# A sparse-attention and mixing kernel: the order of all five instruction streams written by a list scheduler of its own, and GpSimd's pieces halved

## The chip, the cores and the metric

One core of a Trainium2 chip runs the whole program. The metric is the device time of one execution in microseconds (us), the median of several runs. The engines have these names: PE (TensorE, matmuls and transposes), PEld (its weight loads, which overlap with matmuls), DVE (VectorE), ACT (ScalarE), POOL (GpSimd), and SP, whose queue issues DMAs.

## The reference, cut to what matters

```python
scores = q @ k.T / sqrt(64)                  # 8 batches, 8 heads, 576 x 576
thresh = max(scores, -1) - tau
attn = softmax(where(scores >= thresh, scores, -1e9))
x = concat_heads(attn @ v)                   # (8, 576, 512)
theta = x @ w_theta                          # 512 x 512
zr, zi = x * cos(theta), x * sin(theta)
u = x + w_tok_r @ zr + w_tok_i @ zi          # over the 576 tokens
out = u + relu(u @ w_ch)                     # 512 x 512
```

The four weight matrices arrive as eight-byte numbers, all else as float32.

## The kernel before, in words

**Attention.** Two heads of one batch form a pair; there are 32 pairs, four for each batch. A pair is worked in nine halves: four tiles of 128 query rows for either head, and a ninth that holds the last 64 rows of both. A half is a chain over three engines. PE makes the scores `s_ps` (L288: four matmuls of 288 columns, ten in the ninth half). `s_ps` has one buffer, so the next scores wait until DVE has copied these to `sc` (L292, which takes the row maximum on the way). A small addition makes the threshold (L306 on POOL for batches 0 and 1, L310 on DVE later), ACT takes the exponential (L314), and DVE masks and sums (L318). PE transposes the half (L344, four transposes, and L359, a fifth for the last 64 keys of every second half) into a PSUM bank of the pool `ps_t` with its six banks, ACT copies that to `a` (L349), and after four and after nine halves PE multiplies with `v` (L379, two groups of 20 instructions). `normalize` spreads the reciprocals of the row sums over partitions (L395) and multiplies them on (L401). The products want float32 accuracy, so `q`, `k`, `x`, `u` and `z` are split into a rounded high part and a low part, the difference. The low parts of `q` (L238) and `k` (L114, tile k) are made on POOL but for the first pair, those of `x` and `u` (L114, tiles xl and ul) on POOL for three chunks in four and on DVE for the fourth.

**Mixture.** For every batch, once its four pairs are there: `angle` (L423, tiles m_ps<-xh and xl; four chunks m of 24 matmuls), `sines` (L485 to L508: the absolute value on DVE, two sines on ACT between two table loads, the products with x on POOL as L507), `flip` (L519, transposes with a high and a low part, L521 and L522), `token` (L536, four chunks of 54 matmuls), `split_u`, and the last product (L423, tiles m_ps<-uh and ul) with its eviction L584 and the store L589. `ORDER` sets the steps.

**Weights.** `load_weight` turns the eight-byte numbers of 17 chunks (four of `w_theta`, nine of the two token matrices, four of `w_ch`) into high and low parts with five DVE instructions (L142 to L151), and three matmuls (L166 to L168) for 13 of the chunks. The pieces of `w_theta` and `w_ch` go to DRAM and come back through `get_wm` (L202), a DMA on POOL's queue.

**What sets the order.** PE's order is written out by hand: the main loop at the end starts the scores of a half three halves ahead (`AHEAD`), and `fill` puts in so much of the mixture of the batch before that it is spread evenly over the 36 halves of a batch (`share`). The other engines' orders come from the framework's scheduler by priorities (`ATTENTION`, `SINES`) and estimates of its own.

Of the kernel before, what the change touches and what calls it, by code (L numbers as in the profile page):

```python
# [39 lines left out]
def tile_attn_moe(  # L40
# [17 lines left out]
    SP = S + 64  # L58
    NK = 9

# [4 lines left out]
    ps_t = ctx.enter_context(tc.tile_pool(name="ps_t", bufs=6, space=PSUM))  # L65

    @contextmanager
    def at(offset, step=1):

        here = tc.cur_priority  # L70
        tc.cur_priority = max(0, here + offset)
        yield
        tc.cur_priority = here + step
# [3 lines left out]

# [11 lines left out]
    span = small[:, 2 : 3]  # L89
    nc.vector.tensor_scalar(out=gate, in0=tau_sb, scalar1=0.0, scalar2=1.0 / root, op0=ALU.is_ge, op1=ALU.mult)  # L90
    nc.vector.tensor_scalar(out=span, in0=tau_sb, scalar1=0.0, scalar2=BIG, op0=ALU.is_lt, op1=ALU.mult)
    nc.vector.tensor_tensor(out=span, in0=tau_sb, in1=span, op=ALU.add)
    half_pi = small[:, 3 : 4]
    nc.vector.memset(half_pi, 0.5 * math.pi)
# [5 lines left out]
    def pool_copy(out, in_):  # L100
        nc.gpsimd.tensor_scalar(out=out, in0=in_, scalar1=1.0, scalar2=0.0, op0=ALU.mult, op1=ALU.add)

    def copy(eng, out, in_):
        if eng is nc.scalar:
            nc.scalar.copy(out=out, in_=in_)  # L105
        elif eng is nc.gpsimd:
            pool_copy(out, in_)
        else:
            eng.tensor_copy(out=out, in_=in_)  # L109

    def split(eng_hi, eng_lo, hi, lo, src):

        copy(eng_hi, hi, src)
        eng_lo.tensor_tensor(out=lo, in0=src, in1=hi.bitcast(F32), op=ALU.subtract)  # L114

    def temp(name, dt=F32):
        return pool.tile([P, S], dt, tag="t576", name=name, bufs=4)

    def after(ins, other):

        info = mybir.DependencyInfo(mybir.DependencyClass.NoSync, mybir.DependencyReason.DATA)
        tc.add_manual_dep(ins.ins, other.ins.name, info, reason="order")
        return ins

    turn = [0, 0]
    table = SimpleNamespace(back=None, exps=[])

    def load_weight(src, n, places, on_pe):

        raw_tag = turn[0] % 2  # L130
        turn[0] += 1
        tag, bufs = ("z", 3) if raw_tag else ("wm", 3)
        raw = pool.tile([P, S, 2], U32, tag=tag, name="wraw", bufs=bufs)[:, :n]
        nc.sync.dma_start(raw, src.bitcast(U32).rearrange("p (n t) -> p n t", t=2))
        low, high = raw[:, :, 0], raw[:, :, 1]
        w = pool.tile([P, S], F32R if on_pe else F32, tag="xh", name="w", bufs=4)[:, :n]
        bits = pool.tile([P, S], U32, tag="xh", name="bits", bufs=4)[:, :n]
        mag = pool.tile([P, S], U32, tag="xl", name="mag", bufs=4)[:, :n]
        magf, bitsf = mag.bitcast(F32), bits.bitcast(F32)
        yield  # L140
        nc.scalar.activation(out=magf, in_=high.bitcast(F32), func=AF.Abs)
        nc.vector.tensor_scalar(out=magf, in0=magf, scalar1=W_LEAST, scalar2=W_MOST, op0=ALU.max, op1=ALU.min)  # L142
        yield
        nc.vector.tensor_scalar(
            out=bits, in0=mag, scalar1=3, scalar2=0x3FFFFFFF, op0=ALU.logical_shift_left, op1=ALU.bitwise_and
        )
        nc.vector.scalar_tensor_tensor(
            out=bits, in0=high, scalar=0xC0000000, in1=bits, op0=ALU.bitwise_and, op1=ALU.bitwise_or
        )
        nc.vector.tensor_scalar(out=mag, in0=bits, scalar1=0xFF800000, scalar2=None, op0=ALU.bitwise_and)  # L150
        nc.vector.scalar_tensor_tensor(out=w, in0=low, scalar=2.0**-52, in1=magf, op0=ALU.mult, op1=ALU.mult)  # L151
        if not on_pe:
            nc.vector.tensor_tensor(out=w, in0=w, in1=bitsf, op=ALU.add)
            yield
            hi, lo = places()
            split(nc.scalar, nc.vector, hi, lo, w)
            return
        yield

        hi, lo = places()  # L160
        nc.scalar.copy(out=hi, in_=bitsf)
        n2 = n if n <= 512 else n // 2
        for c in range(0, n, n2):
            r = slice(c, c + n2)
            ps = ps_t.tile([P, 512], F32, tag="t", name="w_ps")[:, :n2]
            nc.tensor.matmul(ps, ident, bitsf[:, r], start=True, stop=False)  # L166
            nc.tensor.matmul(ps, one, w[:, r], start=False, stop=False)
            nc.tensor.matmul(ps, minus, hi[:, r], start=False, stop=True)  # L168
            nc.scalar.copy(out=lo[:, r], in_=ps)

    def load_wtok(c):
        yield from load_weight(w_tok[c * P : (c + 1) * P, :], S, lambda: (wt_h[:, c], wt_l[:, c]), True)

    def load_wm(which, src, c):
        kept = []

        def places():
            kept.extend(
                pool.tile([P, DM], F32R, tag="zh4" if x == "whi" else "zl4", name=x, bufs=4) for x in ("whi", "wlo")
            )  # L180
            return kept

        yield from load_weight(src[c * P : (c + 1) * P, :], DM, places, which == 0)
        for i, t in enumerate(kept):
            nc.sync.dma_start(
                wm_dram[which, :, :, i, c, :].rearrange("m p e -> p m e"),
                t.bitcast(F32).rearrange("p (m e) -> p m e", e=P),
            )

    def all_loads(todo):  # L190
        for fn, a in todo:
            yield from fn(*a)

    loads = [(load_wm, (0, w_theta, c)) for c in range(NM)]
    loads += [(load_wtok, (c,)) for c in range(NK)]
    streams = [all_loads(loads[i::2]) for i in range(2)]

    late = all_loads([(load_wm, (1, w_ch, c)) for c in range(NM)])

    def get_wm(which, m):  # L200
        t = pool.tile([P, 2, NM, P], F32R, tag="wm", name=f"wm{which}", bufs=3)
        nc.gpsimd.dma_start(t, wm_dram[which, m].bitcast(F32R))  # L202
        return t

    qq_t = []
    for i in range(2):
        qq = const.tile([P, S + SP], F32R, name=f"qq{i}")
        nc.gpsimd.memset(qq[:, S:SP].bitcast(F32), 0.0)
        qq_t.append(qq)
# [6 lines left out]

    xT = {}
    pairs = {}

    def load_raw(n, src, name, j):  # L220
        raw = temp(name)
        for r in (slice(0, 64), slice(64, P)):
            nc.sync.dma_start(raw[r], src[n // NP, n % NP, :, j])
        return raw

    def prepare_q(n, heads=(0, 1)):

        if 0 in heads:
            pairs[n] = SimpleNamespace(n=n, b=n // NP, p=n % NP, keys=[], a={})
        pr = pairs[n]  # L230
        pr.qf = qq_t[n % 2]
        for j in heads:
            raw = load_raw(n, qT, f"qraw{n}", j)
            qq = pr.qf[:, SP * j : SP * j + S]
            nc.scalar.activation(out=raw, in_=raw, func=AF.Copy, scale=gate)  # L235
            nc.scalar.copy(out=qq, in_=raw)  # L236
            eng = nc.gpsimd if n else nc.vector
            eng.tensor_tensor(out=qq[64:128], in0=raw[64:128], in1=qq[64:128].bitcast(F32), op=ALU.subtract)  # L238

# [62 lines left out]
    def softmax(u, j):  # L302
# [12 lines left out]
        if table.back is not None:  # L315
            after(ins, table.back)
# [409 lines left out]
```

## Time and profile before

| what | value |
|---|---|
| median of 3 runs | 1108.44 us (1106.35 to 1109.0) |
| the profiled execution | 1106.87 us, its span from first to last instruction 1105.1 us |
| first scores copied, first matmul of a mixture | 9.1 us, 135.58 us |
| from one batch's first `sc` to the next, batches 2 to 6 | 128.3 to 129.2 us |
| after the last `sc` | 81.5 us |
| granted clock of TensorE, mean | 0.995 of full speed |

The profiled execution's own time is 1.8 us above its span. The stages below are bounded by the first `sc` of a batch: 9.1, 122.8, 255.1, 383.8, 512.1, 641.3, 769.8, 898.2 us, and the last one at 1023.6 us. From the second stage on each stage holds the attention of one batch and most of the mixture of the batch before; after 1023.6 us only mixtures are left.

### The profile page before, as it was taken

What the parts mean: (1) busy time and instruction counts of PE and PEld (TensorE: products, weight loads), DVE (VectorE), ACT (ScalarE), POOL (GpSimd) and SP (SyncE); (2) the same over time, 40 slices, a digit from 0 to 9 for tenths busy, and PEclk for the clock granted to TensorE, in tenths of its full rate; (3) what the DMA queues carried; (4) which work ended last, traced back from release to release, by engine and by line L of the source; (5) the groups of instructions that cost most, each with busy time, mean ns of one, the idle gap of its engine ahead of it and who ended that gap; (6) DMA issues with size and microseconds to landing.
All of it is one profiled execution on the core that took longest, in us unless ns stands there. A gap on an engine that the chain in (4) does not pass through costs nothing.

```text
span 1105.1 us, 21156 instructions
## 1 busy us (share of the span) xinstructions
PE 1030.0 (93%) x7736; PEld 913.7 (83%) x7736; DVE 844.8 (76%) x2070; ACT 740.4 (67%) x1402; POOL 426.8 (39%) x375
## 2 busy tenths in 40 slices
PE   4888899899999999999999999999999999899998
PEld 3666688698788888888878988898888888788898
DVE  6898787976886679767887778876797668877472
ACT  6788878566786568765686667964687656864350
POOL 3345645444352343532363243522435323630210
PEclk9999999999999999999999999999999999999999
DMA  8632222345221243314232152212432143300411
GB/s 267 198 109 87 76 79 84 98 131 169 84 85 55 67 147 101 87 34 125 90 100 66 33 173 80 85 54 70 145 106 82 33 134 98 90 28 1 138 58 62
DMA packets 55175, 105.25 MB, mean 95 GB/s; under 512 B 11936, under 2 KB 20128, under 8 KB 55072
## 3 DMA queue, kind: packets, MB, share of 16 engines
q1 hardware_dynamic: 45856, 70.35, 21.3%
q0 software_dynamic: 9216, 33.56, 10.3%
q8 instruction: 61, 1.00, 0.4%
q14 instruction: 42, 0.34, 0.1%
HBM read 90.24 MB, written 13.63 MB: 94 GB/s over the span
## 4 chain that ended last, share of the span: by engine, by line
PE 64%; DVE 14%; ACT 10%; issue 5%; POOL 3%; DMA 2%; SPq 0%; POOLq 0%; ACTq 0%; DVEq 0%
PE y_ps L536 16%; PE m_ps L423 14%; PE s_ps L288 12%; PE o_ps L379 10%; PE t_ps L344 7%; DVE sc L292 3%; DVE s_sb L318 3%; DVE th L474 2%; PE z_ps L519 2%; ACT s_sb L314 1%; ACT qraw L235 1%; POOL k L114 1%; POOL qq L238 1%; PE t_ps L359 1%; DMA qraw<-in_qT_dram 1%
## 5 line engine op out<-in xcount | busy, mean ns | idle before, releaser
L318 DVE SCALAR_TENSOR_TENSOR s_sb<-sc,nm,s_sb 128x576 f32<-128x576 f32 x288 | 265.2, 925 | 81.0 <-ACT s_sb L314 70.7
L314 ACT ACTIVATE s_sb<-sc,nm 128x576 f32<-128x576 f32 x288 | 223.8, 780 | 103.7 <-DVE sc L292 102.8
L288 PE MATMUL s_ps<-k,qq 128*128 128x288 f32 (+1 forms) x1344 | 240.0, 306 | 52.1 <-DVE sc L292 34.0
L292 DVE TENSOR_SCALAR_CACHE_REDUCE sc<-s_ps 128x576 f32<-128x576 f32 x288 | 216.9, 753 | 68.8 <-PE s_ps L288 64.6
L288 PEld LDWEIGHTS s_ps<-k,qq 128*128 128x128 f32 x1344 | 194.1, 192 | 79.5 <-DVE sc L292 43.6
L349 ACT COPY a<-t_ps 128x512 f32<-128x512 f32 x256 | 148.5, 580 | 61.0 <-PE t_ps L344 60.2
L344 PE MATMUL t_ps<-ident,s_sb 128*128 128x128 f32 x1152 | 175.3, 275 | 0.8 <-DVE zl L522 0.8
L379 PE MATMUL o_ps<-a,v 128*64 128x320 f32 (+1 forms) x1280 | 170.0, 411 | 1.0 <-ACT a L349 0.8
L536 PE MATMUL y_ps<-wt_h,zh 128*128 128x288 f32 x576 | 164.7, 304 | 1.2 <-ACT zh L521 1.2
L536 PE MATMUL y_ps<-wt_l,zh 128*128 128x288 f32 x576 | 163.3, 302 | 0.0
L114 POOL TENSOR_TENSOR k<-kraw,k 128x576 fp32r<-128x576 f32 x62 | 93.9, 1515 | 165.2 <-ACT k L105 163.6
L344 PEld LDWEIGHTS t_ps<-ident,s_sb 128*128 128x128 f32 x1152 | 142.6, 142 | 1.5 <-DVE zl L522 1.0
L379 PEld LDWEIGHTS o_ps<-a,v 128*64 128x64 f32 x1280 | 86.4, 136 | 62.7 <-issue 6.4
L238 POOL TENSOR_TENSOR qq<-qraw,qq 64x576 fp32r<-64x576 f32 x62 | 99.8, 1612 | 60.0 <-ACT qq L236 29.2
L536 PEld LDWEIGHTS y_ps<-wt_h,zh 128*128 128x128 f32 x576 | 108.7, 189 | 1.7 <-ACT zh L521 1.7
L536 PEld LDWEIGHTS y_ps<-wt_l,zh 128*128 128x128 f32 x576 | 108.9, 189 | 0.0
L202 POOL DMA_DIRECT2D wm<-wm_dram x64 | 36.3, 568 | 179.2 <-PE m_ps L423 144.5
L536 PE MATMUL y_ps<-wt_h,zl 128*128 128x288 f32 x576 | 103.2, 305 | 0.0
L507 POOL TENSOR_TENSOR z<-z,xT 128x576 f32<-128x576 f32 x56 | 84.3, 1536 | 20.3 <-ACT z L494 20.1
L423 PE MATMUL m_ps<-xh,wm 128*128 128x288 f32 x512 | 90.6, 303 | 0.3 <-ACT xh L105 0.3
L114 POOL TENSOR_TENSOR ul<-xT,uh 128x576 fp32r<-128x576 f32 x24 | 34.8, 1448 | 132.5 <-DVE uh L109 89.2
L423 PE MATMUL m_ps<-uh,wm 128*128 128x288 f32 x512 | 84.0, 299 | 0.0
(89 smaller groups left out, 1663.9 us busy)
## 6 DMA issues: line engine op xcount, KB each, us to landing
wm<-wm_dram POOLq DMA_DIRECT2D x64, 512.0 KB, 3.7
qraw<-in_qT_dram SPq DMA_DIRECT2D x128, 144.0 KB, 3.0
kraw<-in_kT_dram SPq DMA_DIRECT2D x128, 144.0 KB, 2.9
out_dram<-xT SPq DMA_DIRECT2D x32, 288.0 KB, 2.1
v<-in_vp_dram SPq DMA_DIRECT2D x32, 256.0 KB, 2.7
wraw<-in_w_tok_dram SPq DMA_DIRECT2D x9, 576.0 KB, 4.3
wraw<-in_w_theta_dram SPq DMA_DIRECT2D x4, 512.0 KB, 6.5
wm_dram<-whi SPq DMA_DIRECT2D x8, 256.0 KB, 2.4
```

The lines of the kernel that those rows point to most:

```text
L114: eng_lo.tensor_tensor(out=lo, in0=src, in1=hi.bitcast(F32), op=ALU.subtract)
L238: eng.tensor_tensor(out=qq[64:128], in0=raw[64:128], in1=qq[64:128].bitcast(F32), op=ALU.subtract)
L288: nc.tensor.matmul(ps[:, h, d0:d1], st, kk, start=(x == 0), stop=(x == len(todo) - 1))
L292: nc.vector.tensor_scalar(out=sc.rearrange("p (a b) -> p a b", a=2), in0=ps[:, :, :HS], scalar1=-1.0, scalar2=None, op0=ALU.mult, op1=ALU.min,
L314: ins = nc.scalar.activation(out=e, in_=u.ps[j], func=AF.Exp, bias=nm[:, j : j + 1], scale=-1.0)
L318: nc.vector.scalar_tensor_tensor(out=e, in0=u.ps[j], scalar=nm[:, 2 + j : 3 + j], in1=e, op0=ALU.is_le, op1=ALU.mult, accum_out=u.pr.rows[ ...
L344: nc.tensor.transpose(out=tp[:, c * P : (c + 1) * P], in_=u.sf[:, k0 + c * P : k0 + (c + 1) * P], identity=ident)
L349: nc.scalar.copy(out=t.a[:, :, j, q0 : q0 + P], in_=tp.rearrange("p (c q) -> p c q", c=4))
L379: nc.tensor.matmul(o[64 * j : 64 * j + 64, :w], st, mv, start=(c == 0), stop=(c == 4))
L423: nc.tensor.matmul(tiles[h][:, :HS], wm[:, a, c, :], parts[c][bb][:, hs], start=(count[h] == 0), stop=(count[h] == 11))
L507: lo_eng.tensor_tensor(out=zi, in0=zi, in1=x, op=ALU.mult)
L536: nc.tensor.matmul(ps[:, :HS], z, w, start=(n == 0), stop=(n == len(work) - 1))
```

## The change

Every piece of work becomes an `Op` with its engine, a duration, a key (when it is wanted, counted in halves) and the buffers that it reads and writes. `Plan.run` goes through time: of the operations that are ready on an engine within 0.04 us of the earliest it takes the one with the lowest key, and emits all five engines' instructions in that order. The table `AT` holds the keys' offsets. A rule `held_up` adds to the key of an operation of DVE or POOL (those marked `lock`) that would collide with one of the other. Buffers have explicit slots; `s_ps` still has one, `ps_t` still six banks, and raws, row reciprocals and the halves of the `w` chunks share three buffers.

What moves between engines: the low parts of `k` and `u`, two of four of `x`, and those of `q` for pairs 0 to 5 go to DVE, and so do the 72 small additions of POOL (L306). POOL keeps the low parts of `q` from pair 6 on, two of four of `x`, and the products with the sines of batches 0 to 6, each as two instructions of 288 columns. ACT takes all of the evictions to `th` (two chunks of four were DVE's, L465). The absolute value becomes a bit operation. The 64 loads of `get_wm` go from POOL's queue to SP's. The four chunks of `w_ch` are added up on PE as the others are.

```diff
-AHEAD = 3
-ATTENTION, SINES = 20, 10000
-LAG = 3
+SEM = 0.06
+TABLE = 1.29
+AT = {
+    "wait": 0.04, "margin": 0.0, "held": 2.51,
...
+    "pq": 26, "px": 2, "pu": 0, "pz": 7, "pk": 0, "ta": 4, "cut": 2,
+}
+def ON_POOL(what, n, j):
+    if what == "q":
+        return n >= 32 - AT["pq"]
+    if what == "k":
+        return j < AT["pk"]
+    if what == "x":
+        return j < AT["px"]
+    if what == "u":
+        return j < AT["pu"]
+    return n < AT["pz"]
...
+class Plan:
...
+    def run(self):
...
+        while todo:
+            best = None
+            for e in range(5):
+                got = [(t, o) for o in cand[e] if forced[e] in (None, o) and (t := begin(o)) is not None]
...
+                t0 = min(t for t, _ in got)
+                _, t, o = min(((o.key + AT["held"] * held_up(o, t, AT["margin"]), o.n), t, o) for t, o in got if t <= t0 + AT["wait"])
+                if best is None or t < best[0]:
+                    best = (t, o)
...
+        self.ops.sort(key=lambda o: (o.start, o.n))
+        for o in self.ops:
+            o.fn()
...
+    def low(on_pool, out, in0, in1, key, R, W, n=S):
...
+        (b, p), k = W, AT["cut"]
+        if on_pool:
+            for i in range(k):
+                gps(c_pool(n // k), lambda i=i: go(nc.gpsimd, S * i // k, S * (i + 1) // k), key, R, ((b, (p, i)),))
+        else:
+            dve(c_two(n), lambda: go(nc.vector), key, R, ((b, [(p, i) for i in range(k)]),), lock=True)
...
-        nc.gpsimd.dma_start(t, wm_dram[which, m].bitcast(F32R))
+        load(lambda: nc.sync.dma_start(t().bitcast(F32), wm_dram[which, m]), key, (wm_b[which],), (t,), 512)
...
-    with tc.manual_schedule(engines={nc.tensor.engine}):
...
+    with tc.manual_schedule(engines={e.engine for e in (nc.tensor, nc.vector, nc.scalar, nc.gpsimd, nc.sync)}):
+        plan.run()
```

**SP's queue at the start.** Before, the `k` of the second head of pair 0 is the fourth load:

```order
L223 DMA qraw_97<-in_qT_dram 64x576 x2
L223 DMA kraw_103<-in_kT_dram 64x576 x2
L223 DMA qraw_110<-in_qT_dram 64x576 x2
L223 DMA kraw_116<-in_kT_dram 64x576 x2
L134 DMA wraw<-in_w_theta_dram 128x1024
```

Now:

```order
L477 DMA raw<-in_qT_dram 64x576 x2
L477 DMA raw<-in_kT_dram 64x576 x2
L477 DMA raw<-in_qT_dram 64x576 x2
L510 DMA v<-in_vp_dram 128x512
L513 DMA v_91<-in_vp_dram 64x64 x2
L366 DMA wm<-in_w_theta_dram 128x1024
L510 DMA v<-in_vp_dram 128x512
L513 DMA v_93<-in_vp_dram 64x64 x2
L477 DMA raw<-in_kT_dram 64x576 x2
```

The second head's `k` has moved behind the `v` of two pairs and the first chunk of `w_theta`.

**DVE where the third mixture begins**, some 400 us into the program. Before, the low part of the fourth chunk of `x` (xl, L114) stands between two `sc`, and a mask (L318) follows ahead of the next `sc`:

```order
L292 TENSOR_SCALAR sc,nm<-s_ps 128x576
L114 TENSOR_TENSOR xl<-xT_4605,xh 128x576
L310 TENSOR_SCALAR nm<-nm,small 128x1
L318 SCALAR_TENSOR_TENSOR s_sb,rows_4670<-sc,nm,s_sb 128x576
L292 TENSOR_SCALAR sc,nm<-s_ps 128x576
L318 SCALAR_TENSOR_TENSOR s_sb,rows_4670<-sc,nm,s_sb 128x576
```

Now, at the same place, with the scores of the same pair:

```order
L578 SCALAR_TENSOR_TENSOR s_4936,rows<-sc,nm,s_4936 128x576
L347 TENSOR_TENSOR xl<-xT,xh 128x576
L558 TENSOR_SCALAR sc,nm<-s_ps 128x576
L347 TENSOR_TENSOR xl<-xT,xh 128x576
L566 TENSOR_SCALAR nm<-nm,small 128x1
L578 SCALAR_TENSOR_TENSOR s_5030,rows<-sc,nm,s_5030 128x576
L558 TENSOR_SCALAR sc,nm<-s_ps 128x576
L566 TENSOR_SCALAR nm<-nm,small 128x1
L578 SCALAR_TENSOR_TENSOR s_5030,rows<-sc,nm,s_5030 128x576
L558 TENSOR_SCALAR sc,nm<-s_ps 128x576
L347 TENSOR_TENSOR k<-raw,k 128x576
```

There are two low parts of `x` now, one ahead of and one behind the `sc`, and a low part of `k` follows.

**PE at that place.** Before, only three matmuls with xl stand between a transposed half and the next scores, and these three need a low part:

```order
L423 MATMUL m_ps<-xh,wm_4945 128x288 x12
L344 MATMUL t_ps<-ident,s_sb 128x128 x4
L359 MATMUL t_ps<-ident,s_sb 128x128
L423 MATMUL m_ps<-xl,wm_4945 128x288 x3
L288 MATMUL s_ps<-k_12_1_4528,qq_87 128x288
```

Now:

```order
L745 MATMUL m_ps<-xh,wm 128x288 x9
L550 MATMUL s_ps<-k,qq_87 128x288 x4
L745 MATMUL m_ps<-xh,wm 128x288 x3
L745 MATMUL m_ps<-xl,wm 128x288 x6
L597 MATMUL t_ps<-ident,s_5030 128x128 x4
L745 MATMUL m_ps<-xh,wm 128x288 x2
L745 MATMUL m_ps<-xl,wm 128x288
L550 MATMUL s_ps<-k,qq_87 128x288 x6
```

The scores have moved into the middle of the matmuls with xh, and the six with xl stand together behind them.

## Rows read from the trace of the kernel before

**Rows 1.** The page's first part: busy us of each engine, its share of the span, and instructions.

```profile
PE 1030.0 (93%) x7736; PEld 913.7 (83%) x7736; DVE 844.8 (76%) x2070; ACT 740.4 (67%) x1402; POOL 426.8 (39%) x375
```

**Rows 2.** Busy time by stretch. The columns: stretch in us, its length, busy us of PE, PEld, DVE, ACT and POOL with their instructions, granted clock, DMA share, GB/s.

```profile
9.00:122.80 113.80, 91.45 (x564) 70.92 (x564) 98.63 (x224) 92.52 (x180) 55.20 (x58) 0.99 0.52 158
122.80:135.58 12.78, 10.82 (x76) 8.00 (x75) 10.20 (x28) 12.16 (x26) 7.06 (x8) 1.00 0.25 71
135.58:255.10 119.52, 110.48 (x824) 98.30 (x823) 98.44 (x215) 79.17 (x148) 56.66 (x62) 0.97 0.32 93
...
255.10:1023.60 768.50, 740.15 (x5713) 663.52 (x5712) 594.11 (x1519) 526.13 (x999) 293.24 (x223) 1.00 0.29 87
...
383.80:512.10 128.30, 123.72 (x958) 111.06 (x957) 99.20 (x255) 88.61 (x168) 50.19 (x38) 1.00 0.30 89
...
1000.00:1020.00 20.00, 20.00 (x156) 18.18 (x156) 14.41 (x39) 8.76 (x19) 1.42 (x1) 1.00 0.00 1
...
1023.60:1105.10 81.50, 75.54 (x563) 71.98 (x562) 41.13 (x79) 25.33 (x45) 13.35 (x15) 0.99 0.28 88
```

**Rows 3.** Links of the chain that ended last, from 1000 us on, where PE is never idle: start in us, length in us, engine, tile, line, and how many instructions are merged.

```profile
1002.03 0.44 PE t_ps L344 x4
1002.58 0.79 PE y_ps L536 x6
...
1005.91 2.84 PE o_ps L379 x20
1008.76 0.59 PE rb_ps L395 x4
1009.45 0.53 PE s_ps L288 x4
...
1019.92 2.31 PE o_ps L379 x20
1022.23 1.35 PE s_ps L288 x10
...
1088.47 12.75 PE m_ps L423 x96
```

**Rows 4.** What PE waited for in the stage from 383.8 to 512.1 us: us in total, times, longest.

```profile
PE s_ps L288 <- DVE sc L292: 1.9, 3, 0.9
PE t_ps L359 <- DVE zl L522: 1.1, 1, 1.1
PE s_ps L288 <- POOL k L114: 1.0, 1, 1.0
PE rb_ps L395 <- DVE km L468: 0.6, 1, 0.6
```

**Rows 5.** The timeline where the third mixture begins, from three answers (PE, DVE, POOL): start in us, length, engine, line, and in brackets the idle time before with what ended it.

```profile
403.96 0.92 PE L423 MATMUL m_ps<-xl,wm 128*128 128x288 f32 x3
405.80 0.80 PE L288 MATMUL s_ps<-k,qq 128*128 128x288 f32 x4 [0.91 <-DVE sc L292]
...
401.14 1.95 DVE L114 TENSOR_TENSOR xl<-xT,xh 128x576 fp32r<-128x576 f32 x1
...
403.13 1.93 DVE L318 SCALAR_TENSOR_TENSOR s_sb<-sc,nm,s_sb 128x576 f32<-128x576 f32 x1
...
406.71 0.82 DVE L318 SCALAR_TENSOR_TENSOR s_sb<-sc,nm,s_sb 128x576 f32<-128x576 f32 x1
...
403.00 1.43 POOL L114 TENSOR_TENSOR xl<-xT,xh 128x576 fp32r<-128x576 f32 x1
```

**Rows 6.** Groups of DVE instructions over the whole run, shapes kept apart: busy us, mean ns of one, idle us before them.

```profile
L318 DVE SCALAR_TENSOR_TENSOR s_sb<-sc,nm,s_sb 128x576 f32<-128x576 f32 x288 | 265.2, 925 | 81.0 <-ACT s_sb L314 70.7 <-POOL nm L306 5.0 <-ACT qraw L235 0.5
...
L310 DVE TENSOR_SCALAR nm<-nm,small 128x1 f32<-128x1 f32 x216 | 44.8, 208 | 2.4
...
L114 DVE TENSOR_TENSOR xl<-xT,xh 128x576 fp32r<-128x576 f32 x8 | 17.0, 2129 | 1.2 <-ACT xh L105 1.2
...
L114 DVE TENSOR_TENSOR ul<-xT,uh 128x576 fp32r<-128x576 f32 x8 | 6.1, 759 | 0.3
...
L150 DVE TENSOR_SCALAR mag<-bits 128x512 uint32<-128x512 uint32 x8 | 3.4, 419 | 0.0
```

**Rows 7.** Groups of DVE instructions from 9 to 135.58 us: the three one-input steps of the weights' conversion, the same columns.

```profile
L144 DVE TENSOR_SCALAR bits<-mag 128x576 uint32<-128x576 uint32 (+1 forms) x13 | 7.7, 591 | 1.1 <-PE w_ps L166 1.1
L142 DVE TENSOR_SCALAR mag<-mag 128x576 f32<-128x576 f32 (+1 forms) x13 | 7.1, 544 | 2.4 <-ACT mag L141 2.4
L150 DVE TENSOR_SCALAR mag<-bits 128x576 uint32<-128x576 uint32 (+1 forms) x13 | 7.0, 537 | 0.1
```

**Rows 8.** The start: busy time from 10 to 15 us (columns as in rows 2), and the fourth load in SP's queue (start and length of its issue).

```profile
10.00:15.00 5.00, 2.54 (x7) 1.90 (x8) 4.29 (x9) 2.81 (x4) 1.01 (x2) 1.00 0.96 243
...
4.95 1.24 SPq L223 DMA_DIRECT2D kraw<-in_kT_dram  x2
```

**Rows 9.** The timeline of PE where a converted chunk of 512 columns is added up, with what follows it.

```profile
44.48 1.02 PE L166 MATMUL w_ps<-bits,ident 128*128 128x512 f32 x2
...
45.80 0.60 PE L344 MATMUL t_ps<-ident,s_sb 128*128 128x128 f32 x4
```

**Rows 10.** The timeline where the last mixture begins: DVE's low part of `x`, and PE behind POOL's.

```profile
1040.86 3.67 DVE L114 TENSOR_TENSOR xl<-xT,xh 128x576 fp32r<-128x576 f32 x1 [1.03 <-ACT xh L105]
...
1043.96 0.80 PE L423 MATMUL m_ps<-xl,wm 128*128 128x288 f32 x4 [0.95 <-POOL xl L114]
```

More of the change, by code (lines that the diff above doesn't have):

```diff
@@ L27 @@
 W_MOST = 122880.0 - 2.0**-7
-AHEAD = 3
-ATTENTION, SINES = 20, 10000
-LAG = 3
-ORDER = "a0 a1 s01 a2 a3f0 s23 t0f1 t1f2 t2f3 t3"
+PE, DVE, ACT, POOL, SP = range(5)
+SEM = 0.06
+TABLE = 1.29
+AT = {
+    "wait": 0.04, "margin": 0.0, "held": 2.51,
+    "theta": 4.0, "theta_by": 4.33, "tok": 24.0, "tok_by": 1.7, "ch": 52.0, "ch_by": 3.89,
+    "q": -7.95, "k": -7.06, "raw": -2.0, "v": -4.0, "m0": 5.11, "m1": 4,
+    "score": -1.5, "nm": -1.4, "add": -1.39, "exp": -2.3, "mask": -1.0, "wrap": -1.58, "turn": -0.16, "copy": 0.05, "last": 0.06,
+    "v0": 4.5, "v1": 9.2, "vcopy": 1.1, "div": 9.4, "rows": -2.22, "rb": -1.5, "dmul": 0.16,
[3 rows of a table added]
+}
@@ new lines, with __init__, __call__ @@
+class Buf:
+    def __init__(self, cls, make, psum=False):
+        self.cls, self.make, self.psum = cls, make, psum
+        self.writers, self.readers = {}, {}
+        self.left, self.slot, self.ap, self.end = 0, None, None, 0.0
+        if cls is not None:
+            cls.queue.append(self)
+    def __call__(self):
+        if self.ap is None:
+            self.ap = self.make(f"{self.cls.name}{self.slot}" if self.cls else None)
+        return self.ap
+class Op:
+    def __init__(self, n, eng, occ, tail, fn, key, lock, mode):
+        self.n, self.eng, self.occ, self.lat, self.fn, self.key = n, eng, occ, occ + tail, fn, key
+        self.lock, self.mode = lock, mode
+        self.deps, self.after, self.bufs = {}, [], []
+        self.start, self.left, self.ready, self.kb, self.then = None, 0, 0.0, 0.0, None
@@ L116, in temp @@
[L116 to L188, printed above, removed]
@@ L215, in tile_attn_moe, with sb, bank, fixed @@
         v5_t.append(v5)
+    plan = Plan()
+    op = plan.op
+    cl = {}
+    for name, n, fifo in (
[3 rows of a table added]
+    ):
+        cl[name] = Class(name, n, fifo)
+    def sb(cls, shape, dt=F32):
+        c = cl[cls]
+        return Buf(c, lambda tag: pool.tile(shape, dt, tag=tag, name=cls, bufs=1))
+    def bank(name):
+        return Buf(cl["t"], lambda tag: ps_t.tile([P, 512], F32, tag=tag, name=name, bufs=1), psum=True)
+    def fixed(ap):
+        b = Buf(None, None)
+        b.ap = ap
+        return b
@@ new lines, in values, with products @@
+    def values(n, g, key):
+        pr = pairs[n]
+        w = 256 if g == 0 else 320
+        a, x = pr.a[g], xT[n]
+        o = bank("o_ps")
+        def products():
+            for c in range(5):
+                for j in range(2):
+                    st = pr.v()[:, 4 * j + c, :] if c < 4 else pr.v5()[:, j, :]
+                    mv = a()[:, 2 * c + j] if c < 4 else a()[:, 8]
+                    nc.tensor.matmul(o()[64 * j : 64 * j + 64, :w], st, mv, start=(c == 0), stop=(c == 4))
+        pe(10 * w / 1200, products, key, (a, pr.v, pr.v5), (o,), mode="v")
+        act(
+            c_act(w, True), lambda: nc.scalar.copy(out=x()[:, 256 * g : 256 * g + w], in_=o()[:, :w]), key + AT["vcopy"], (o,), ((x, g),)
+        )
@@ L562, in moe @@
-                left -= 1
-            elif what == "s":
-                sines(ms)
-            elif what == "f":
-                yield from flip(m)
-            else:
-                other = flip(ms[1]) if turns else iter(())
-                for n, cost in enumerate(token(m)):
-                    yield cost
-                    if n % 5 == 2:
-                        yield next(other, 0)
-                for cost in other:
-                    yield cost
-                done.append(m)
-            while left == 0 and done:
-                split_u(done.pop(0))
@@ new lines, in attention @@
+    def attention(b):
+        for n in range(b * NP, (b + 1) * NP):
+            t = 9 * n
+            pr = pairs[n]
+            for j in range(2):
+                prepare_q(n, j, t + AT["q"] + j)
+                prepare_k(n, j, t + AT["k"] + j)
+            load_v(n, t + AT["v"])
+            pr.rows = sb("rows", [P, 10])
+            pr.a = [sb("a0", [P, 9, 256]), sb("a1", [P, 9, 320])]
+            xT[n] = sb("xT", [P, S])
+            for i in range(9):
+                half(t + i)
+            values(n, 0, t + AT["v0"])
+            values(n, 1, t + AT["v1"])
+            divide(n, t + AT["div"])
@@ L682 @@
+    for b in range(B):
+        attention(b)
+        mix(b)
+    with tc.manual_schedule(engines={e.engine for e in (nc.tensor, nc.vector, nc.scalar, nc.gpsimd, nc.sync)}):
+        plan.run()
 def kernel(**inputs):
```

1023 lines of the change are left out of this document (628 added, 395 removed), and 5 rows, old and new, of tables (AT, cl).

## The prediction

> **What bounds the kernel now.** I read the page's busy shares first, then the busy time by stretch, then the chain that ended last, and then what PE waited for in one stage. The shares say PE: 1030 of 1105.1 us, with DVE at 845 and ACT at 740 [rows 1]. That is one figure for stages with different limits. By stretch [rows 2] there are three regimes. Up to 135.58 us, where the first mixture's matmuls begin, PE is busy for 102.3 of 126.6 us after the first 9, and DVE for 98.63 + 10.20 = 108.8 us: attention alone and the conversion of the weights lie on DVE. From 255.1 to 1023.6 us the six full stages have PE at 740 of 768.5 us. At the end mixtures alone are left, with PE at 75.5 of 81.5 us.
>
> A busy PE says little about how much is to be had, so I work out what a full stage needs when PE is fed, from a part of the chain in which it never waits [rows 3]. Four score matmuls take 0.53 us and the ten of a ninth half 1.35; four transposes with the change of kind after them 0.44; the fifth adds 1002.58 - 1002.03 - 0.44 = 0.11; the products with v 2.31 and 2.84; the reciprocals 1009.45 - 1008.76 = 0.69; and 96 matmuls of 288 columns 12.75, that is 0.133 each. A pair needs 8 x 0.53 + 1.35 + 9 x 0.44 + 5 x 0.11 + 5.15 + 0.69 = 15.9 us, four of them 63.8. A mixture needs 192 + 216 = 408 matmuls x 0.133 = 54.2 us, and 8 x 0.44 + 4 x 0.11 = 4.0 for its flips. Together 121.9 us against the 128.3 that a stage takes: 6.4 us lost in each, and 38 in the six. Of these 768.5 - 740.15 = 28.4 us are seen as idle, the rest hides under the modelled tails of matmuls.
>
> A second way to the same number is a rule of the Trainium skill. Its page "Perfetto Trace Analysis" (Identifying the Most-Contended Engine) says that matmul busy time misjudges how near a kernel is to its limit, and that weight-load busy time is the better measure. Taken against 100%, PEld with 111.06 of 128.3 us [rows 2] would promise 17 us per stage and some 1000 us in all. But in the 20 us in which PE is busy without a gap, PEld is busy for 18.18 [rows 2]; 91% is full here, and 111.06 / 0.91 gives 122 us, so the rows bear the smaller gain out.
>
> **Where the 6.4 us go.** In the stage from 383.8 us PE is held up by six events: three scores that wait for DVE's copy, a transpose that waits for a bank that DVE's zl frees late, scores that wait for POOL's k, and reciprocals behind DVE's km [rows 4]. One of them shows how: scores stand ready behind three matmuls, but DVE takes 1.95 us for a low part of x and, with POOL's next one running from 403.00, 1.93 us for a mask that takes 0.82 at 406.71; PE waits 0.91 us [rows 5]. These are collisions: DVE's xl takes 2129 ns in the mean where the same shape (ul) takes 759, and all masks lose 925 - 820 = 105 ns, 30 us in all [rows 6].
>
> **The change, part by part.**
>
> *Full stages.* The new order answers each of the six events: at that place the scores stand ahead of the matmuls that need low parts, k is DVE's, and POOL's instructions are halved, so that a collision lasts half as long. POOL's 18 low parts and products of a stage (8 of k's and 3 of u's leave it, and one of x) make 18 x 1.43 = 26 us instead of 50.19 [rows 2, 5]. DVE gains 8 + 3 + 1 low parts x 0.759 = 9.1 us and gives up two evictions of each of two chunks and half the absolute values, some 3.5 us, and about half of what collisions cost, some 4; so it stays near 100 us in a shorter stage, 81% instead of 77%. It is no new bound, but has no slack to spend on a plan that goes wrong. ACT gains four evictions, 1.6 us on 88.6. The bounds for six stages are 0 and -38. I take -31, five sixths: the events are few and each has a cause that the new order removes, while five queues in fixed order will make some small waits of their own.
>
> *Up to the first mixture.* On both sides 43 halves are scored ahead of it. DVE gains 20 low parts up to there (12 of q and 11 of k where 2 and 2 were, 2 of x where 1 was) x 0.759 = 15.2 us, and 42 small additions at something below 0.208 [rows 6], say 6. POOL has nothing to do, so the collisions go: 13 x (0.591 + 0.544 + 0.537 - 3 x 0.419) = 5.4 us in the conversions alone [rows 6, 7]. DVE's work becomes 108.8 + 15.2 + 6 - 6 = 124 us in the time after the first 9, in which it has 126.6 - 108.8 = 17.8 us of idle now. At the very start it loses something: the second head's k moves behind about 1.1 MB of other loads, at 243 GB/s some 4 us, in a stretch where the DMA engines are at 0.96 [rows 8]; conversions fill part of that. With 4 us of idle in all, the first mixture begins at 9 + 124 + 4 = 137 us, +1.5. The bounds are 133 without idle (-2.5) and 151 with today's idle (+15). PE and ACT have room there, so I stay near the lower end.
>
> *The first stage with a mixture, 135.58 to 255.1 us.* 9.0 us of idle are seen [rows 2], with the hidden share of the full stages 12; I take -11. Four chunks of w_ch are now added up on PE, 45.80 - 44.48 = 1.3 us each [rows 9], +5. Together -6, between -7 and +5.
>
> *The end.* 81.5 - 75.5 = 6 us of idle, of which nearly 4 are the last eviction and store. The last mixture's begin shows the same collision, a low part of 3.67 us on DVE and PE waiting behind POOL's [rows 10]; now POOL and DVE have two each and 48 matmuls of the batch before cover them. -2, between -4 and +2.
>
> *At nothing:* the loads of `get_wm` on SP's queue. There they stand among stores that wait for DVE; if their three buffers ahead were used up, matmuls would wait for a transfer, which belongs to the fourth rival.
>
> **The sum.** +1.5 - 31 - 6 - 2 = -37.5 us on the profiled span of 1105.1, that is 1067.6, and with the 1.8 us around it 1069 us. The median of the runs is 1.6 us above the profiled execution, within their spread; I leave that out. About 0.3% (3.3 us) is what a measurement of this kernel can tell from no change.
>
> **The rivals.**
>
> 1. *PE is fed nearly everywhere*: all of the 38 us, 7 at the first mixture, 4 at the end and 2.5 at the start: 1055 us, and down to 1046 if the need per stage is 1% less than I worked out. For it speaks that the lost events are so few; against it that a wait of 0.1 us at each of 245 scores already takes 25 us.
> 2. *Small gain*: DVE, at 81% and ahead of the single score buffer in every half, makes half of the lost time again as new waits (-19), the start keeps today's idle (+15), and the first mixture gives nothing: 1100 us, the case from 1081 to 1105. For it: DVE has as much to do in a shorter time, and k, made on POOL while DVE did other work, is now on the path. Against it: masks and low parts of 0.8 us are shorter than the 1.9 us that hold it up now.
> 3. *No change at all*, if the order as built differs from the old one only where nobody waits. The rows of both orders speak against it.
> 4. *Slower*: the plan and the chip drift apart. A score stands in PE's queue at the instant at which the plan expects DVE's copy; everything behind it waits, whether ready or not. If the copy comes late by 0.25 us in the mean, the 245 scores after the first mixture lose 61 us, where my forecast leaves 7 + 1 + 1 lost there: 1069 + 61 - 9 = 1121 us. The point from which it is slower than before is a mean of (38 + 9) / 245 = 0.19 us. The old hand-written order has the same dependence and 2 us collisions, which speaks against it; that no slack is left for an error in a duration speaks for it.
>
> **Chances.** The forecast, 1058 to 1081 us: 0.58. Rival 1: 0.15. Rival 2: 0.15, nearly all of it faster by over 0.3%. Rival 3, with the edge of rival 2: 0.03. Rival 4: 0.09. So faster 0.87, the same 0.04, slower 0.09. The range from 1046 to 1098 takes in rival 1 with its lower bound, and most of rival 2; it leaves out the slower case and a few hundredths at either end.
>
> **What would show it.** Right: stages of 123 to 125 us from one batch's first `sc` to the next; DVE's masks near 0.84 us in the mean, and no DVE instruction on 576 columns over 1.6 us; the first m_ps between 133 and 141 us; POOL near 200 us in all. Wrong: waits of PE for `sc` above 40 us after the first mixture (rivals 2 and 4), PE waiting for `wm` or raw loads behind a store (rival 4), a first m_ps after 145 us (rival 2), or stages of 122 us (rival 1).

## The result, and the profile after

The changed kernel takes 1063.52 us (median of four runs, 1063.09 to 1064.48), the kernel before in the same session 1107.65 us: a ratio of 0.9603, 95% interval 0.9586 to 0.9619. The profiled span is 1062.7 us against 1105.1. The forecast was 1069 us.

The busy shares first, to be held against [rows 1]:

```profile
PE 1025.7 (97%) x7752; PEld 910.0 (86%) x7752; DVE 850.4 (80%) x2206; ACT 755.8 (71%) x1438; POOL 232.0 (22%) x259
```

PE does the same work and 16 matmuls more (the four chunks of `w_ch`) in 42 us less; POOL's share has nearly halved, DVE's has risen from 76 to 80%. The stretches of [rows 2], cut at the same events (first `sc`, first mixture's matmul, first `sc` of the third batch, last `sc`), with one full stage:

```profile
9.98:139.08 129.10, 108.30 (x671) 79.31 (x672) 120.72 (x318) 107.20 (x209) 3.59 (x4) 0.97 0.49 149
139.08:246.88 107.80, 107.17 (x813) 95.76 (x812) 93.11 (x239) 83.13 (x157) 28.28 (x30) 1.00 0.34 103
246.88:982.55 735.67, 733.60 (x5708) 661.73 (x5707) 593.16 (x1564) 535.50 (x1019) 194.71 (x210) 1.00 0.30 90
370.40:493.40 123.00, 122.32 (x953) 110.09 (x952) 99.27 (x264) 90.38 (x172) 33.15 (x36) 1.00 0.31 92
982.55:1062.70 80.15, 74.93 (x563) 72.18 (x562) 40.36 (x80) 24.92 (x46) 4.11 (x4) 1.00 0.28 89
```

Six full stages gained 768.50 - 735.67 = 32.8 us, and PE's idle in them fell from 28.4 to 2.1 us. The first stage with a mixture gained 11.7; the first mixture begins 3.5 us later; the end gained 1.35. Where [rows 4] has six waits in a single stage, what PE waited for in all six stages is now one line (us in total, times, longest):

```profile
PE t_ps L597 <- ACT s L573: 1.7, 3, 0.6
```

DVE's and POOL's groups (columns as in [rows 6]) show what became of the collisions:

```profile
L578 DVE SCALAR_TENSOR_TENSOR s<-sc,nm,s 128x576 f32<-128x576 f32 x288 | 254.2, 883 | 48.6 <-ACT s L573 46.4
...
L347 DVE TENSOR_TENSOR xl<-xT,xh 128x576 fp32r<-128x576 f32 x48 | 43.5, 910 | 0.9 <-ACT xh L706 0.5
```

```profile
L347 POOL TENSOR_TENSOR qq<-raw,qq 64x288 fp32r<-64x288 f32 x104 | 105.3, 1033 | 396.1 <-ACT qq L491 278.9 <-PE t_ps L622 56.6 <-issue 53.1
L832 POOL TENSOR_TENSOR z<-z,xT 128x288 f32<-128x288 f32 x112 | 94.5, 881 | 116.3 <-ACT z L813 114.4 <-issue 1.9
```

Masks are down from 925 to 883 ns, DVE's xl from 2129 to 910. The two have different causes: with POOL's pieces whole again (run e3 below) the masks are back at 933 ns, so their gain goes with the short pieces, while DVE's xl stays short, at 802 ns, so there the new order is enough. A POOL piece of 288 columns takes 881 to 1033 ns: clearly over half of the 1.43 us that a whole one took [rows 5].

### The profile page after: what moved, and what is told of

Its sections match the earlier page's. It is cut to its first block, busy times and chain, and to the rows that moved or that the text cites. A ratio compares the mean times of both kernels' runs of the same rounds, so it can differ in the third digit from the quotient of the medians.

```text
span 1062.7 us, 21251 instructions
## 1 busy us (share of the span) xinstructions
PE 1025.7 (97%) x7752; PEld 910.0 (86%) x7752; DVE 850.4 (80%) x2206; ACT 755.8 (71%) x1438; POOL 232.0 (22%) x259
## 4 chain that ended last, share of the span: by engine, by line
PE 83%; ACT 9%; DVE 6%; issue 2%; SPq 0%; DMA 0%; ACTq 0%
PE y_ps L886 19%; PE m_ps L745 17%; PE o_ps L650 15%; PE s_ps L550 14%; PE t_ps L597 11%; PE z_ps L857 2%; ACT s L573 2%; DVE s L578 2%; DVE sc L558 1%; PE t_ps L622 1%; PE rb_ps L681 1%; ACT z L813 1%; ACT L817 1%; ACT L810 1%; PE w_ps L427 1%
## 5 line engine op out<-in xcount | busy, mean ns | idle before, releaser
L578 DVE SCALAR_TENSOR_TENSOR s<-sc,nm,s 128x576 f32<-128x576 f32 x288 | 254.2, 883 | 48.6 <-ACT s L573 46.4
L573 ACT ACTIVATE s<-sc,nm 128x576 f32<-128x576 f32 x288 | 223.0, 778 | 88.6 <-DVE sc L558 87.1
L597 PE MATMUL t_ps<-ident,s 128*128 128x128 f32 x1152 | 177.8, 277 | 15.2 <-DVE s L578 12.5
L347 POOL TENSOR_TENSOR qq<-raw,qq 64x288 fp32r<-64x288 f32 x104 | 105.3, 1033 | 396.1 <-ACT qq L491 278.9
L745 PE MATMUL m_ps<-xh,wm 128*128 128x288 f32 x1024 | 177.6, 301 | 0.3 <-ACT xh L706 0.3
L597 PEld LDWEIGHTS t_ps<-ident,s 128*128 128x128 f32 x1152 | 136.3, 141 | 35.4 <-DVE s L578 16.4
L745 PEld LDWEIGHTS m_ps<-xh,wm 128*128 128x128 f32 x1024 | 146.7, 188 | 2.0 <-ACT xh L706 0.8
L832 POOL TENSOR_TENSOR z<-z,xT 128x288 f32<-128x288 f32 x112 | 94.5, 881 | 116.3 <-ACT z L813 114.4
L745 PE MATMUL m_ps<-xl,wm 128*128 128x288 f32 x512 | 95.9, 303 | 0.0
L886 PEld LDWEIGHTS y_ps<-wt_h,zl 128*128 128x128 f32 x576 | 81.7, 189 | 4.7 <-issue 4.6
```

Of the source, the lines that this page charges most:

```text
L347: eng.tensor_tensor(out=out()[:, c0:c1], in0=in0()[:, c0:c1], in1=in1()[:, c0:c1], op=ALU.subtract)
L573: lambda: nc.scalar.activation(out=s()[:, j], in_=sc(), func=AF.Exp, bias=nm()[:, j : j + 1], scale=-1.0),
L578: lambda: nc.vector.scalar_tensor_tensor(out=s()[:, j], in0=sc(), scalar=nm()[:, 2 + j : 3 + j], in1=s()[:, j], op0=ALU.is_le, op1=ALU.mul ...
L597: nc.tensor.transpose(out=tp()[:, c * P : (c + 1) * P], in_=sf()[:, k0 + c * P : k0 + (c + 1) * P], identity=ident)
L745: nc.tensor.matmul(ps[h]()[:, :HS], wm()[:, a, c, :], parts[c][bb]()[:, h * HS : (h + 1) * HS], start=first and n == 0, stop=final and n = ...
L832: eng.tensor_tensor(out=zi, in0=zi, in1=x[m]()[:, c0:c1], op=ALU.mult)
```

## The experiments

Each row of this table is one kernel; times are in us, and stages are from one batch's first `sc` to the next. "Last w_ps" is when PE adds up the last converted chunk of weights (all four of `w_ch` for the changed kernel).

| kernel | median us | ratio to before (interval) | first m_ps | last w_ps | third batch's first sc | its stage | mean of the next four |
|---|---|---|---|---|---|---|---|
| before | 1107.65 | 1 | 135.6 | 106.7 | 255.1 | 128.7 | 128.6 |
| after | 1063.52 | 0.9603 (0.9586-0.9619) | 139.1 | 223.5 | 246.9 | 123.5 | 123.2 |
| e1, old places | 1098.12 | 0.9894 (0.9864-0.9925) | 138.0 | 271.4 | 250.4 | **149.0** | 124.0 |
| e2, old order | 1106.14 | 0.9964 (0.9954-0.9975) | 141.6 | 107.4 | 262.0 | 127.4 | 127.5 |
| e3, whole pieces | 1084.11 | 0.9768 (0.9749-0.9787) | 138.4 | 253.2 | 243.9 | **138.4** | 124.4 |
| e4, PE's order alone | 1240.11 | 1.1171 (1.1140-1.1202) | 201.8 | 302.4 | 327.7 | 142.5 | 139.8 |
| f1, four raw buffers | 1089.46 | 0.9831 (0.9808-0.9854) | 135.3 | 261.6 | 245.6 | **145.6** | 124.0 |
| f2, whole, four raw | 1101.82 | 0.9935 (0.9917-0.9952) | 140.0 | 260.7 | 253.4 | **141.3** | 126.1 |
| f3, plan 0.25 us off | 1093.59 | 0.9867 (0.9842-0.9891) | 140.8 | 260.8 | 245.8 | **145.9** | 125.0 |
| f4, no low z | 1084.98 (one run) | - | 140.6 | 231.0 | 244.3 | 133.5 | 127.2 |
| g1, late w_ch | 1085.67 | 0.9786 (0.9763-0.9809) | 138.3 | 262.3 | 238.7 | **153.8** | 123.3 |
| g2, f1 with early w_ch | 1078.97 | 0.9725 (0.9696-0.9755) | 138.1 | 225.8 | 256.8 | 123.8 | 124.0 |
| g3, e1 with early w_ch | 1078.22 | 0.9721 (0.9696-0.9745) | 137.5 | 230.9 | 256.7 | 124.1 | 124.1 |
| g4, e3 with early w_ch | 1073.90 | 0.9681 (0.9659-0.9704) | 138.7 | 207.7 | 247.5 | 125.7 | 124.5 |

**First four: which part of the change does it.**

e1 gives the low parts of `q`, `k`, `x` and `u` their old engines under the new order. The small additions, the evictions to `th`, the absolute value, the loads of `get_wm` and the adding up of `w_ch` stay as in the changed kernel:

```diff
-    "pq": 26, "px": 2, "pu": 0, "pz": 7, "pk": 0, "ta": 4, "cut": 2,
+    "pq": 31, "px": 3, "pu": 3, "pz": 7, "pk": 2, "ta": 4, "cut": 2,
```

> The new list scheduler with the old places of the low parts: k on GpSimd, three chunks in four of u and of x, q from pair 1 on; the pieces stay halved. Theory A (the order of the five streams makes the gain, wherever the low parts are): 1064 to 1075 us, full stages of 123 to 125 us. Rival B (taking the low parts from GpSimd makes it): GpSimd has 50 us of work in a stage again, collisions with DVE come back, full stages of 126 to 128 us, 1083 to 1103 us.

e2 makes the reverse edit in the kernel before: the new places of the low parts and of the small additions, and halved pieces, under its hand-written order, as here for `k`:

```diff
-        split(nc.scalar, nc.gpsimd if n else nc.vector, k1, k2, raw)
+        split(nc.scalar, nc.vector, k1, k2, raw)
```

> The kernel before with its own order, but the new places (k, u and half of x on VectorE, q there for pairs 0 to 5, the small additions on VectorE) and GpSimd's instructions halved. Theory A (order): 1095 to 1112 us, full stages of 127 to 129 us. Rival B (places and halves): 1070 to 1085 us, stages of 124 to 125 us.

e3 sets `"cut": 1`, and POOL's pieces are whole again:

> The changed kernel with GpSimd's pieces whole, planned anew. Theory A (the plan knows the collisions and puts them where nobody waits): 1064 to 1068 us, though the masks on VectorE get longer. Rival C (short pieces are what keeps the masks short): masks back at 0.92 us in the mean, full stages of 125 us or more, 1075 to 1085 us.

e4 keeps the changed kernel's PE order and leaves the other four to the framework's scheduler:

```diff
-    with tc.manual_schedule(engines={e.engine for e in (nc.tensor, nc.vector, nc.scalar, nc.gpsimd, nc.sync)}):
+    with tc.manual_schedule(engines={nc.tensor.engine}):
```

> The same work and places, TensorE in the plan's order, the other four engines ordered by the framework's scheduler. Theory A (all five streams have to fit each other): TensorE waits for copies and banks that come in another order than its own, 1085 to 1120 us. Rival D (TensorE's order alone carries the gain, as the others only have to follow it): 1064 to 1072 us.

By the totals alone order (e1, -1.1%) and places (e2, -0.4%) would seem to need each other for the -4%, and halving would be worth 20 us. The stages say otherwise. e1's ordinary stages take 124.0 us, so the order has nearly its full effect there; 25 us went in one stage that takes 149. Under the old order the waits stay: in the six full stages of e2 PE still waits 25.8 us (9.3 for `sc`, 7.2 for DVE's km, 6.7 for zl, 2.6 for k), where the kernel before has 28.3. e3 has one long stage like e1's (138.4); its masks, 933 ns, are as long as its rival C says, but its ordinary stages, 124.4, are not. e4, above the range of either theory, says that a PE order fitted to five streams is worse than the old one if the other streams don't follow it.

**Four more, on the start, that stage, rival 4 and the limit.** f1 gives the shared raw buffers a fourth, f3 lets the planner believe that DVE's copy of a score is 0.25 us shorter:

```diff
-        ("s", 1, True), ("t", 6, False), ("raw", 3, False), ...
+        ("s", 1, True), ("t", 6, False), ("raw", 4, False), ...
```

> One edit in the changed kernel: the shared class of raw loads, conversion halves and spread reciprocals has four buffers of one size instead of three. Theory A (the start lost its 3.5 us because the fourth raw load, the second head's k, waits for a buffer until 9.2 us): the second score is copied near 12 to 13 us instead of 16.8, the first m_ps comes near 136 us instead of 139.1, and the time is some 3 us lower, 1060 to 1061 us. Theory B (DVE, 120.7 us busy of the 129.1 up to the first mixture, is the bound there, whatever comes in first): first m_ps at 138 to 139.5, the time the same, 1063 to 1064 us.

The start did what theory A said: the second score is copied at 12.63 us instead of 16.81, the first m_ps comes at 135.3. The time went up by 26 us all the same, in a stage of 145.6 us: one more buffer closed the gap that it was meant for, and the order that the scheduler then wrote lost more elsewhere.

f2 makes this edit and that of e3.

> Whole pieces on GpSimd, as in the run before that gave 1084 us, and the shared raw class with four buffers. That run has six stages of 124.4 us, but one of 138.4 from 243.9 us on, with the last conversions of weights at 253 us. Theory A (that one stage, not the size of the pieces, cost most of the 20 us: there the copy of the reciprocals and the last conversions queue for the three raw buffers, and the second mixture begins late): the long stage falls to about 125, the time to 1067 to 1073 us, and halving is worth only (124.4 - 123.25) x 6 = 7 us plus a little. Theory B (the long pieces themselves hold DVE up, there as everywhere): the stage stays over 133 us and the time between 1079 and 1086 us.

A miss: the stage stays at 141.3 and the time lies above both ranges, so one more buffer of that class does not shorten the stage. (Its later stages alternate between 123.6 and 128.6; why stays open.)

```diff
-            c_ps(S) + 0.083,
+            c_ps(S) + 0.083 - 0.25,
```

> One edit in the changed kernel: the planner takes DVE's copy of a score as 0.25 us shorter than it is; on the chip it takes what it took. Theory A (slack in the queues and the planner's own order absorb most of it): full stages of 124 to 127 us, time 1068 to 1090 us. Theory B (the fourth rival: each score of the 245 stands where the plan expects its copy, so 0.25 us is lost at each): full stages near 132 us, time near 1063.5 + 61 = 1125 us.

The mechanism of rival 4 costs 125.0 - 123.2 = 1.8 us a stage, not 8 to 9; most of the 30 us is again in the one stage, of 145.9. The time fell between the two ranges.

f4 leaves the products with the low part of z out of `token`, and out of the count by which the mixture is spread:

```diff
-                work += [(c, 1, wt_h, "h") for c in range(NK)]
...
-        total = (16 * 3 * 4 * 131 + 36 * 110 + 72 * 393) / 1000
+        total = (16 * 3 * 4 * 131 + 36 * 110 + 48 * 393) / 1000
```

> Leaves out one of the three products of the last matrix multiplication of every mixture, the one with the low part of z (72 matmuls of 288 columns a batch, 72 x 0.133 = 9.6 us of PE); the low part is still made, by DVE. Theory A (the full stages are bound by PE alone now): stages of 113.5 to 114.5 us, 8 x 9.6 = 77 us in all, 985 to 990 us. Theory B (DVE, 99 us of 123, or the fixed order is nearly the bound as well): stages over 117 us, 1015 us or more.

With 9.6 us of PE work taken away the stages are longer, 127.2 us in the mean, as theory B allowed. This rests on a single execution, and here too the scheduler wrote a new order. Two stretches of f4 (columns as in [rows 2]), one with PE fed and one in a later stage where the next z are made:

```profile
580.00:600.00 20.00, 20.00 (x162) 18.46 (x159) 13.96 (x36) 11.25 (x23) 1.57 (x2) 1.00 0.10 30
...
690.00:710.00 20.00, 16.35 (x91) 12.59 (x91) 16.45 (x39) 17.44 (x31) 9.41 (x10) 0.74 0.16 45
```

In the second ACT and DVE make sines and z, PE is busy for 16.35 of 20 us, and its granted clock is 0.74 in the mean, part of the time at the lower of its two levels. So a stage is not bound by PE alone; how much of the loss is the clock and how much the order, this run does not show.

**The one long stage.** In all five kernels with such a stage the last chunk of `w_ch` is converted behind the third batch's first `sc` (e1: 271.4 against 250.4 us), in the changed kernel ahead of it (223.5 against 246.9). g1 moves only that due time, by one number:

```diff
-    ... "ch": 52.0, "ch_by": 3.89,
+    ... "ch": 52.0, "ch_by": 4.6,
```

> One number in the changed kernel: the four chunks of w_ch get due times 4.60 apart instead of 3.89 (first one as before, 52.0). In the order that comes out of it the last chunk is converted after the second batch's first outputs, as in the five variants that lost 14 to 25 us in one stage. Theory A (that loss is the late last conversion: it holds the buffers of raw, xh and xl that the second batch's division and mixture need, and the first batch's last product needs its weights): the stage from 247 us on takes 140 to 150 us instead of 123.5, the other stages stay at 123 to 124, the time is 1080 to 1092 us. Theory B (the loss comes from elsewhere in those plans): the stages as they were, 1062 to 1067 us.

Theory A held, with a stage even longer: 153.8 us. Three views of g1 show how: ACT's timeline at the casts into the shared raw buffers, SP's queue at the same time, and the stretches (columns as in [rows 2]).

```profile
249.55 0.59 ACT L433 CAST raw<-w_ps 128x512 fp32r<-128x512 f32 x1 [1.05 <-DMA wm_dram<-raw]
252.54 0.62 ACT L419 CAST raw<-xh 128x512 fp32r<-128x512 f32 x1 [2.41 <-DMA wm_dram<-raw]
255.53 0.59 ACT L433 CAST raw<-w_ps 128x512 fp32r<-128x512 f32 x1 [2.38 <-DMA wm_dram<-raw]
258.77 0.62 ACT L672 COPY raw<-rows 128x512 f32<-128x512 f32 x1 [2.65 <-DMA wm_dram<-raw]
```

```profile
247.18 19.41 SPq L455 DMA_DIRECT2D wm_dram<-raw  x6
268.52 1.28 SPq L466 DMA_DIRECT2D wm<-wm_dram  x3
```

```profile
245.00:255.00 10.00, 4.59 (x18) 2.42 (x16) 5.03 (x11) 3.17 (x5) 1.50 (x2) 0.97 0.38 109
255.00:265.00 10.00, 5.56 (x17) 3.55 (x17) 5.27 (x14) 2.45 (x5) 0.00 (x0) 0.52 0.20 54
265.00:275.00 10.00, 8.91 (x66) 6.83 (x66) 7.21 (x20) 6.86 (x13) 0.00 (x0) 1.00 0.62 200
```

Each cast waits until the store of the one before has left its buffer, 3 us apiece; behind them in ACT's order stands the copy of the reciprocals (L672), without which there is no `x` of the second batch, and the pieces of `w_ch` are loaded (L466) only behind six stores on SP's queue. PE is busy for 4.59 us of the 10 from 245 us on, and in the next 10 its granted clock is 0.52, close to its lower level. In the changed kernel the same casts come between 197 and 225 us with PE fed by the mixture, and the longest idle time before one is 0.28 us.

Not all of this holds for every long stage. Casts or the copy L672 wait for a store in e1 and f1 too, but in e3, f2 and f3 none does. What all six share is the other half: the last product of the first batch, which needs the pieces of `w_ch`, starts at 268 to 283 us (in the changed kernel at 239.6), and PE lacks its matmuls until then; in e3, from 255 to 265 us, PE is busy for 7.29 of 10 us at a granted clock of 0.83. A part of a long stage is also work that has moved into it: PE does 1007 instructions in g1's and 880 in the stage ahead of it, where the changed kernel does 964 and 931, so some 45 matmuls, at 0.133 us each 6 us, have crossed the border.

The last three give three of the long kernels earlier due times:

```diff
-    ... "ch": 52.0, "ch_by": 3.89,
+    ... "ch": 46.0, "ch_by": 3.2,
```

> The run with four raw buffers (1089.5 us, one stage of 145.6 us, the last conversion at 262 us) and due times of w_ch of 46.0 and 3.2 instead of 52.0 and 3.89, by which the last conversion comes before the second batch's first outputs. Theory A: the stage falls to 124 to 126, the last conversion is done before 230 us, and the time is 1089.5 - 21 = 1068 us, 1063 to 1072. Theory B (the fourth buffer itself makes that order worse): the stage stays over 138, 1083 to 1092 us.

> The new order with the operations on the engines of before (1098.1 us, one stage of 149.1, the last conversion at 271 us), pieces halved, and the same earlier due times of w_ch (46.0 and 3.2). Theory A (new places are worth 0.75 us in each of six stages and something at the start; the rest of the 35 us was the late conversion): that stage falls to 124 to 126, time 1098 - 25 = 1073 us, 1069 to 1078. Theory B (the order needs the new places): 1088 to 1100 us.

> Whole pieces on GpSimd (1084.1 us, one stage of 138.4, the last conversion at 253 us), and the same earlier due times of w_ch (46.0 and 3.2). Theory A (halving is worth 1.1 us in each of six stages and little else; the rest was the late conversion): that stage falls to 124.4 to 126, time 1084 - 14 = 1070 us, 1066 to 1074. Theory B (long pieces hold DVE up in that stage too): 1079 to 1086 us.

In all three the long stage is gone (123.8, 124.1, 125.7). g4 is at the top end of its range, g3 just above its own, g2 at 1079 between its two theories: what the stage gives back is partly paid ahead of it (third batch's first `sc` at 256.8 us in g2, at 245.6 in f1), where the work that had moved now stands again (935 PE instructions in that stage, 885 in f1). None beats the changed kernel.

**What each part is worth**, with the long stage out of the way. Order and halving with the low parts at their old places: g3 against before, 2.8%, nearly all in the six full stages, which end 997.00 - 256.68 = 740.3 us after they began instead of 768.5, -28.2 us; what PE waits for there is 3.1 us instead of 28.3. New places: from 124.1 to 123.2 a stage, 4.7 us in six; another 9.8 us lie ahead of the third batch, but these are not shown to be the places' work, since g2, with the new places, four raw buffers and g3's due times, has that `sc` at 256.8 as well. Under the old order the same places with halved pieces gave 1.1 us a stage and lost 6.9 at the start (e2). Halving: g4, whose due times are earlier too, against after, 0.78 of a per cent of before, 8 to 10 us, of them 744.5 - 735.7 = 8.8 in the full stages. The due times of four chunks of weights: 22 us (g1). No run gives back the evictions to `th`, the absolute value or the queue of `get_wm` alone; they count with the order here, and the waits for DVE's km may have gone by the evictions.

## Why the prediction was right, and where it was not

The sum was -37.5 us, measured are 1062.7 - 1105.1 = -42.4. Of the difference of 4.9 us the first mixture's stage makes 5.7, the full stages 1.8, and the start and the end take 2.6 back. The full stages were forecast for the right reason; that the whole is off by no more is partly luck, as errors of both signs cancel.

- **Full stages: -31 predicted, -32.8 measured.** The mechanism was right: the six events of [rows 4] are gone, DVE is at 99.27 of 123.00 us as predicted ("near 100 us in a shorter stage, 81%"), and the need of 121.9 us that came out of [rows 3] is missed by 122.6 - 121.9 = 0.7 us in the mean. The order carries most of it (e1, g3); the prediction had named order, places and halving together and did not divide the gain among them. The second way to that need holds too: in g1's stage from 392.51 us PE has no idle at all and PEld is at 111.68 of 123.43 us, 90%.

```profile
392.51:515.94 123.43, 123.43 (x964) 111.68 (x963) 99.84 (x265) 90.64 (x172) 33.66 (x36) 1.00 0.31 95
```

Taken against 100%, the weight-load busy time by which the Trainium skill's page "Perfetto Trace Analysis" (Identifying the Most-Contended Engine) judges PE would still leave a tenth there; PE was busy throughout, so the measurement decides that 90% is full here.

- **First stage with a mixture: -6 predicted, -11.7 measured**, outside its bounds of -7 to +5. Of it 8.4 us are idle that went (9.04 to 0.63), the +5 for `w_ch` came as 5.93 (x16 matmuls into w_ps), one group of products with v (3.0 us) fell ahead of the stretch. The rest, some 6 us, is PE's own busy time, and no step of the prediction had it. Eight fewer matmuls of m_ps and s_ps in the stretch are 8 x 0.133 = 1.1 of it. Another part stood in [rows 2], where I overlooked it: a granted clock of 0.97 in that stretch, now 1.00, at most 0.03 x 119.52 = 3.6 us. What is left stays open. In the kernel before it is down in two places, with PE busy for 13.72 and 10.73 of 15 us:

```profile
165.00:180.00 15.00, 13.72 (x94) 12.07 (x94) 10.53 (x25) 13.01 (x22) 9.52 (x9) 0.89 0.20 59
...
195.00:210.00 15.00, 10.73 (x65) 8.27 (x66) 14.57 (x30) 7.28 (x14) 7.25 (x6) 0.89 0.37 111
```

- **Up to the first mixture: +1.5 predicted, +3.5 measured.** Work on DVE was 120.7 us where 124 was predicted, idle 8.4 where 4 was, and the first `sc` came 0.9 us later. The second head's k is where the prediction had it: its load is issued at 9.18 us instead of 4.95 [rows 8], and the second `sc` comes at 16.81 instead of 13.31. It stands so far back because of the three shared raw buffers: with a fourth the scheduler puts it in its old place (f1: second `sc` at 12.63, first m_ps at 135.3). But the idle is not shown to be its price: of the 8.4 us only 2.4 fall before 30 us, and f1 has 9.8 us of idle up to its first m_ps, which comes earlier because 5.6 us less of DVE's work stands ahead of it. Where the rest of the idle comes from stays open. The 5.4 us for the conversions were a little too many: 9 of the 13 chunks in [rows 7] have 576 columns, and the 419 ns held against them is for 512.
- **The end: -2 predicted, -1.35 measured.**
- **POOL's pieces** were taken at half of 1.43 us; they take 0.88 to 1.03, so POOL has 33.15 us in a stage instead of 26, and 232 in all instead of 200. The 1.43 was that of one xl; whole pieces of the kernel before took 1443 to 1612 ns in the mean. Masks are at 883 ns instead of 840; no DVE instruction on 576 columns takes over 1.6 us, as predicted (the longest is a mask of 1.43).
- **Rival 4** was priced too high: an error of 0.25 us in the plan costs 1.8 us a stage (f3). From 391.77 us on PE waits for a score's copy there only once, for 0.4 us; most of its waiting is for masks, 4.7 us in all.
- **What no step priced:** `w_ch` was charged 1.3 us a chunk on PE and nothing for its buffers and its place. There lies the largest risk of this change: in five of the first six variants with all five streams planned the conversions came so late that one stage grew by 14 to 25 us. That the table of the changed kernel avoids it, the profile of before could not show.

## What to carry to other kernels

Compare variants stage by stage before any total is read: here 25 us in a single stage made three helpful parts look useless or indispensable. An order from a greedy scheduler answers a small edit with a different order everywhere, so an experiment on one part must check that the rest stayed. One-time work that shares buffers with the steady state needs a due time of its own, and its price is the wait of whatever stands behind it in each queue.

## What was not expected of the hardware

Less PE work went with more time: without 72 of its matmuls a batch, stages were 4 us longer, and the granted clock was down to 0.74 in a stretch of 20 us (f4, one execution, with an order of its own). On POOL two halves cost more than a whole: 2 x 881 against 1546 ns for z, 2 x 1033 against 1480 for qq (e3), yet the stages are 1.1 us shorter with halves:

```profile
L832 POOL TENSOR_TENSOR z<-z,xT 128x576 f32<-128x576 f32 x56 | 84.6, 1546 | 124.2 <-ACT z L813 121.8 <-issue 2.4
L347 POOL TENSOR_TENSOR qq<-raw,qq 64x576 fp32r<-64x576 f32 x52 | 76.9, 1480 | 449.4 <-ACT qq L491 328.1 <-PE t_ps L622 117.0 <-issue 2.2
```
